# Decayed attention and a gelu MLP on one core: second-block state parts as row tiles, and a new order for wave 1

## The chip, the cores and the metric

The kernel runs on one core of a Trainium2 chip. The metric is the device time of one execution in microseconds, as the median over runs. TensorE (PE) multiplies and writes to PSUM; VectorE (DVE), ScalarE (ACT) and GpSimd (POOL) work on SBUF and PSUM; SyncE (SP) issues the DMAs.

## The reference

The input is q, k, v of shape (4, 8, 768, 64) in float32 (batch, heads, tokens, head size), a decay per head, and two weight matrices of 512 × 2048 and 2048 × 512. The output is (3072, 512) in float32.

```python
for b in range(nb):                       # blocks of 64 tokens
    intra = (qb @ kb^T * Dmask) @ vb      # Dmask[i, j] = lam ** (i - j) for i >= j, else 0
    inter = (qb * lam ** (pos + 1)) @ kv_state
    out[:, :, sl] = intra + inter
    kv_state = lam ** 64 * kv_state + (kb * lam ** (63 - pos))^T @ vb
x = out as (3072, 512)                    # heads side by side
h = x @ w_in
y = (h * sigmoid(1.702 * h)) @ w_out
```

## The kernel before, in words

**Waves.** The kernel holds all weights and operands of matmuls in bfloat16 and accumulates in float32. It works through six waves of 512 rows of the MLP's input. Waves 2 to 5 take 128 tokens of all four batches each. The first 256 tokens are split otherwise, so that work can start on few loads: wave 0 takes 256 tokens of batches 0 and 1, wave 1 the same of batches 2 and 3. A *unit* `(bl, p)` of wave 0 or 1 is one batch and one pair of heads, 256 tokens; a wave has 8 units. In wave 1 the four units with bl = 0 are `A_UNITS` and those with bl = 1 are `B_UNITS`. Token pairs are laid out so that partitions 0 to 63 hold the first 128 tokens (even and odd apart) and partitions 64 to 127 the second 128.

**A unit's work.** `u_cast_kq` scales k (on VectorE) and q (on GpSimd) by powers of the decay while casting them; `u_cast_v` casts v; `u_turn` transposes k and q with four TensorE transposes into PSUM and `u_turn_copy` copies them to SBUF; `u_score` (L301) makes 8 score matmuls of 64×64 weights into the two banks of the tile `s`; `u_mask` (L306, VectorE) multiplies by the causal mask; `u_kv0` (L326) makes 4 matmuls for the state after the first half and `u_kv0_copy` (L335, two ScalarE instructions) writes it to `kv_bd`; `u_inter` (L360) is one full-size matmul of q on that state, and `u_out` adds 8 matmuls of v with the masked scores (L369) and copies the result into the transposed MLP input `xT` (L371, ScalarE). For these waves the state that wave 2 starts from needs the second half too: `u_state(w, p)` (L347) makes 8 matmuls on partitions 64 to 127 for one pair of heads and the two batches of one wave, in its own PSUM tile, and adds them to `kv_bd` into `kv_sb[0]` with two VectorE instructions (L350).

**PSUM.** Eight banks: three single tiles `mm` (MLP accumulators, and wave 0's transposes), one tile `s` of two banks, one tile `o` of two banks, one tile `t`. `s`, `o` and `t` have one buffer each, so a new one waits until the readers of the last are done.

**MLP.** `mlp1(w, fc)` makes 4 matmuls (L453) for 128 of the 2048 hidden units, `gelu` (L459, ScalarE) follows; `mlp2(w, g, j)` makes 4 of the 16 matmuls (L484) for 128 output rows; a copy and a store on SP follow the sixteenth. The very last 128 rows go through `mlp2_last` (L500), which splits the 512 columns in two halves, each with its own copy and store.

**Order.** Instructions are issued in the order in which the program emits them, engine by engine; nothing reorders them but the queues themselves. Wave 0 is a loop with one unit per turn, with filler matmuls on zeros (`fill`, L255; counts in `FILL0` and `FILL`) ahead of each unit's transposes. After it, `put` writes a main list of MLP items with due times on a clock of its own (1 is 4 matmuls of 512 columns), and `at` a side list of attention steps; the merging loop at the end emits a side step before the first main item whose time is not below the step's. `units1` places wave 1's units: A from `A_T` in steps of `A_S`, beside wave 0's `mlp1`; B two items apart, beside wave 0's `mlp2`. Round i of it transposes unit i, scores unit i − 1 and finishes unit i − 2. For each unit the casts come half a step ahead of its transposes. `states` places `u_state`: wave 0's in the stretch where `mlp1` of wave 1 runs for the A half of its columns (HA), wave 1's where it runs for the B half (HB). `full` places waves 2 to 5.

**Loads.** All loads are issued by SP into a ring of SBUF chunks; `pump`, called after each step, issues whatever fits next. The order is wave 0's units (first two of 128 KB per tensor, then nine loads of 256 KB, two units each), `w_in`, wave 1's A units, `w_out`, wave 1's B units, then waves 2 to 5. DMA transposes and stores stand in the same SP queue.

Of the kernel before, what the change touches and what calls it, by code (L numbers as in the profile page):

```python
# [24 lines left out]
def kernel(  # L25
# [60 lines left out]
    def load_units(w, nm, bl, p, n=2):  # L86

        def go(x):
            nc.sync.dma_start(  # L89
                out=x.rearrange("s (h c) -> s h c", h=2 * n),  # L90
                in_=SRC[nm][2 * w + bl, 2 * p : 2 * (p + n), 0 : 2 * P, :].rearrange("h (q j) d -> q h (j d)", j=2))
            for i in range(n):
                loaded[w, nm, bl, p + i] = x.rearrange("s (n h j d) -> s n h j d", n=n, h=2, j=2)[:, i]
        coming.append((n, [(w, nm, bl, p + i) for i in range(n)], 1, go))
# [199 lines left out]
    def u_score(w, bl, p):  # L294
        s = ps.tile([P, 2, W], f32, tag="s", name="ps_s")
        s_ps[w, bl, p] = s
        t = kq_of[w, p][:, bl]
        for j in range(2):
            for x in range(2):
                for h in range(2):  # L300
                    nc.tensor.matmul(s[hd(x), h, j * P : (j + 1) * P].rearrange("s (i m) -> s i m", i=2),  # L301
                                     t[hd(h), 0, j, hd(x)], t[hd(h), 1, :, hd(x)], start=True, stop=True)
# [38 lines left out]
    def u_state(w, p):  # L341

        t = ps.tile([P, W], f32, tag="t", bufs=1, name="ps_kv")[:, 0 : 2 * D].rearrange("s (b d) -> s b d", b=2)
        for bl in range(2):
            for h in range(2):
                for j in range(2):
                    nc.tensor.matmul(t[hd(h), bl, :], kqs_of[w, p][hd(1), bl, 0, j, h],  # L347
                                     v_sb[w % 2][hd(1), p, 2 * bl + j, h], start=(j == 0), stop=(j == 1))
        for h in range(2):
            nc.vector.tensor_tensor(kv_sb[0][hd(h), p, 2 * w : 2 * w + 2, :], kv_bd[hd(h), p, 2 * w : 2 * w + 2, h, :],  # L350
                                    t[hd(h)], op=ADD)
# [12 lines left out]
    def u_out(w, bl, p):  # L364
        o, sm = uo_ps.pop((w, bl, p)), sm_of.pop((w, bl, p))
        for j in range(2):
            for x in range(2):
                for h in range(2):
                    nc.tensor.matmul(o[hd(h), x, 0:P], v_sb[w % 2][hd(x), p, 2 * bl + j, h], sm[hd(x), h, j, :],  # L369
                                     start=(x == 0 and j == 0), stop=True, skip_group_check=True)  # L370
        nc.scalar.copy(xT(w)[:, p, 2 * bl : 2 * bl + 2, :], o[:, :, 0:P])  # L371
# [73 lines left out]
    def mlp1(w, fc, kcs=ALLK, bs=ALL):  # L445
        if (w, fc) not in h_ps:
            if (w, fc) == (0, NF):
                h_ps[w, fc] = ps.tile([P, 2, W], f32, tag="s", name="ps_h4")[:, 0, :]
            else:
                h_ps[w, fc] = ps.tile([P, W], f32, tag="mm", bufs=3, name="ps_h")  # L450
# [43 lines left out]
    def mlp2_last(w, g):  # L494

        hw = d_model // 2
        for c in range(2):
            t = ps.tile([P, hw], f32, tag="mm", bufs=3, name="ps_out")
            for fc in range(FFC):
                nc.tensor.matmul(t, g_of[w][:, fc, g * P : (g + 1) * P],  # L500
                                 w_out_sb[fc // CW][:, fc % CW, c * hw : (c + 1) * hw],
                                 start=(fc == 0), stop=(fc == FFC - 1))
            o = op.tile([P, hw], f32, tag="oh", bufs=2, name="o_sb")
            if c == 0:
                nc.vector.tensor_copy(o, t)
            else:
                nc.scalar.copy(o, t)
            store(w, g, o, slice(c * hw, (c + 1) * hw))

    FILL0, FILL = 12, (0, 2, 2, 2, 1, 1, 1, 1)  # L510
    NF = 3
    A_T, A_S = 7, 1.2
    KV_ENG = {i: nc.vector if i in (2, 4, 6) else nc.scalar for i in range(1, 9)}

    with tc.manual_schedule():
# [63 lines left out]
        def units1(t0, units, step, vcast, copier):  # L579
            n = len(units)  # L580
            for i in range(n + 2):
                t = t0 + step * i
                h = t + 0.5 * step
                if i < n:
                    at(t, u_cast_kq, 1, 0, *units[i], nc.vector)
                    at(t, u_cast_kq, 1, 1, *units[i], nc.gpsimd)
                    at(t, u_cast_v, 1, *units[i], vcast)
                if 0 < i:
                    at(h, new_o)
                if i < n:  # L590
                    at(h, u_turn, 1, *units[i])
                if i > 1:
# [3 lines left out]
                if 0 < i <= n:  # L596
                    at(h, u_score, 1, *units[i - 1])
                    at(h, u_mask, 1, *units[i - 1])
                    at(h, u_kv0, 1, *units[i - 1])
                if i > 1:  # L600
                    at(h, u_out, 1, *units[i - 2])
                if 0 < i <= n:
                    at(h, u_kv0_copy, 1, *units[i - 1], nc.scalar)

        def states(t0, w, step):
            for p in range(NP):
                at(t0 + step * p, u_state, w, p)
# [23 lines left out]
        units1(A_T, A_UNITS, A_S, nc.gpsimd, nc.vector)  # L631
# [15 lines left out]
        states(e - 7, 0, 1.6)  # L647
        units1(e + 2, B_UNITS, 2, nc.scalar, nc.scalar)
# [3 lines left out]
        states(e + 0.5, 1, 1.5)  # L652
# [54 lines left out]
```

## Time and profile before

| | |
|---|---|
| median of 8 runs | 220.23 us (219.7 to 223.4) |
| the profiled execution | 220.1 us, span of its instructions 218.1 us |
| TensorE busy | 209.6 us, 96% of the span, granted clock 1.000 |
| VectorE, ScalarE, GpSimd busy | 107.0, 97.1, 29.0 us |
| first full-rate stream of MLP matmuls | from 20.4 us |
| A half of wave 1 beside wave 0's `mlp1` | 28.8 to 41.3 us |
| wave 0's `mlp2` with the B units | 48.7 to 66.1 us |
| B half of wave 1's `mlp1` | 66.1 to 74.4 us |
| last matmul's copy, then last store | 215.00 us, landed at 217.1 us |
| DMA | 40.15 MB, mean 184 GB/s |

How to read it: a busy time is a sum over the whole span and says nothing of where an engine was late. The chain of work that ended last is followed back from the end, each step to what released it. A line of the timeline has start, duration, engine, line of the kernel, operation, output and inputs, shape and count, and in brackets the idle time before it with what ended it. A matmul's duration includes the way through the array and PSUM; what it costs the next one is seen from the distance of their starts.

### The profile page before, as it was taken

Reading aid. Unit: us, or ns where it says so; the run is one execution under the profiler, and the core shown is the slowest. Engines: PE = TensorE matmul, PEld = TensorE weight load, DVE = VectorE, ACT = ScalarE, POOL = GpSimd, SP = SyncE. Lnnn points to the kernel's source line nnn. Section 1 sums busy time; section 2 is a strip of 40 time slices with the busy share of each in tenths; the row PEclk is TensorE's granted clock in tenths of the full one; section 3 lists DMA queues with packets and bytes.
Section 4 is the critical chain, followed back from the end, with each engine's and each line's share of the span. In section 5 each row is a group of like instructions: output and inputs, shape, how many; then the busy total and the mean of one; then the engine's idle time right before and its main releaser. Section 6 shows DMA issues by size and latency. Waiting matters only on the chain.

```text
span 218.1 us, 4497 instructions
## 1 busy us (share of the span) xinstructions
PE 209.6 (96%) x1766; PEld 107.8 (49%) x1766; DVE 107.0 (49%) x237; ACT 97.1 (45%) x203; POOL 29.0 (13%) x62
## 2 busy tenths in 40 slices
PE   7799979899999999999999999999999999999994
PEld 2354434675547755444554444544444454444453
DVE  4796556694316887193572294661483332100120
ACT  4686747774656511165611075611176520377000
POOL 4773052040040000004000040000040000000000
PEclk9999999999999999999999999999999999999999
DMA  5999999999995899899999979679973222200112
GB/s 135 291 328 376 318 321 387 361 271 214 222 186 107 157 216 200 198 252 192 185 220 186 232 161 219 143 144 191 237 153 73 45 78 75 96 0 0 48 51 96
DMA packets 96741, 40.15 MB, mean 184 GB/s; under 512 B 77136, under 2 KB 89680, under 8 KB 96720
## 3 DMA queue, kind: packets, MB, share of 16 engines
q1 hardware_dynamic: 96576, 39.86, 76.9%
q8 instruction: 14, 0.23, 0.4%
q14 instruction: 7, 0.06, 0.1%
q10 hardware_dynamic: 144, 0.00, 0.0%
HBM read 27.27 MB, written 6.29 MB: 154 GB/s over the span
## 4 chain that ended last, share of the span: by engine, by line
PE 82%; DMA 8%; SPq 5%; ACT 1%; DVE 1%; issue 1%; POOL 0%
PE ps_out L484 37%; PE ps_h L453 33%; DMA ring<-in_moe_w_in_dram 5%; SPq L89 4%; DMA ring<-in_q_dram 3%; PE ps_o L431 2%; PE ps_s L394 2%; PE ps_out L500 2%; PE ps_kv L409 1%; PE ps_o L424 1%; PE ps_t L280 1%; PE ps_kv L347 1%; PE ps_s L301 1%; PE ps_o L369 1%; ACT kv_bd L335 1%
## 5 line engine op out<-in xcount | busy, mean ns | idle before, releaser
L453 PE MATMUL ps_h<-xT,w_in 128*128 128x512 bf16 (+1 forms) x448 | 87.9, 349 | 0.3 <-ACT g_sb L459 0.3
L459 ACT ACTIVATE g_sb<-ps_h 128x512 bf16<-128x512 f32 (+1 forms) x112 | 59.5, 536 | 59.3 <-PE ps_h L453 58.0
L484 PE MATMUL ps_out<-w_out,g_sb 128*128 128x512 bf16 x368 | 83.1, 379 | 0.0
L453 PEld LDWEIGHTS <-w_in 128*128 128x128 bf16 x448 | 42.1, 98 | 37.8 <-issue 0.4
L484 PEld LDWEIGHTS <-g_sb 128*128 128x128 bf16 x368 | 34.8, 98 | 39.0
L491 DVE COPY o_sb<-ps_out 128x512 f32<-128x512 f32 x19 | 13.1, 691 | 52.6 <-PE ps_out L484 49.8
L401 DVE SCALAR_TENSOR_TENSOR sm<-ps_s,inv_pow,mask 128x512 bf16<-128x512 f32 x32 | 22.6, 747 | 22.9 <-PE ps_s L394 22.8
L383 POOL CAST v_sb<-ring 128x512 bf16<-128x512 f32 x16 | 9.8, 651 | 102.2 <-DMA ring<-in_v_dram 66.8
L434 ACT CAST xs<-ps_o 128x512 bf16<-128x512 f32 x16 | 9.4, 586 | 29.2 <-PE ps_o L431 29.2
L306 DVE TENSOR_TENSOR sm<-ps_s,mask 128x512 bf16<-128x512 f32 x16 | 11.0, 688 | 10.7 <-PE ps_s L301 10.7
L263 POOL TENSOR_TENSOR kqs<-ring,kq_pow 128x256 bf16<-128x256 f32 x16 | 10.3, 660 | 28.5 <-DMA ring<-in_q_dram 26.0
L413 DVE SCALAR_TENSOR_TENSOR kv<-kv,blk,ps_kv 64x256 bf16<-64x256 bf16 x24 | 11.4, 474 | 0.2
L381 DVE TENSOR_SCALAR kqs<-ring,k_pow 128x256 bf16<-128x256 f32 x32 | 11.2, 391 | 0.2
L381 DVE TENSOR_SCALAR kqs<-ring,q_pow 128x256 bf16<-128x256 f32 x32 | 11.1, 390 | 0.0
L280 PE MATMUL ps_t<-ident,kqs 128*128 128x128 bf16 x64 | 6.8, 221 | 2.8 <-POOL kqs L263 1.9
L255 PE MATMUL ps_f<-zeros 128*128 128x512 bf16 x22 | 8.1, 488 | 1.3 <-DVE zeros L177 1.3
L263 DVE TENSOR_TENSOR kqs<-ring,kq_pow 128x256 bf16<-128x256 f32 x16 | 7.7, 491 | 3.1 <-ACT kq_pow L208 1.9
L288 ACT COPY kq<-ps_t 128x512 bf16<-128x512 bf16 x10 | 5.9, 587 | 6.8 <-PE ps_t L280 6.8
L280 PEld LDWEIGHTS <-kqs 128*128 128x128 bf16 x64 | 4.6, 98 | 7.7 <-DVE kqs L263 2.9
L350 DVE TENSOR_TENSOR kv<-kv_bd,ps_kv 64x128 bf16<-64x128 bf16 x16 | 4.6, 285 | 7.8 <-PE ps_kv L347 7.4
L371 ACT CAST xT<-ps_o 128x256 bf16<-128x256 f32 x16 | 6.0, 372 | 2.9 <-PE ps_o L369 2.6
L150 DVE CAST w_out<-ring 128x512 bf16<-128x512 f32 x16 | 7.1, 493 | 0.1
(66 smaller groups left out, 118.2 us busy)
## 6 DMA issues: line engine op xcount, KB each, us to landing
ring<-in_k_dram SPq DMA_DIRECT2D x23, 256.0 KB, 4.8
ring<-in_q_dram SPq DMA_DIRECT2D x23, 256.0 KB, 4.6
ring<-in_v_dram SPq DMA_DIRECT2D x23, 256.0 KB, 4.6
ring<-in_moe_w_in_dram SPq DMA_DIRECT2D x16, 256.0 KB, 5.9
ring<-in_moe_w_out_dram SPq DMA_DIRECT2D x16, 256.0 KB, 5.3
out_dram<-o_sb SPq DMA_DIRECT2D x15, 256.0 KB, 2.3
out_dram<-o_sb SPq DMA_DIRECT2D x18, 128.0 KB, 2.6
ring<-in_k_dram SPq DMA_DIRECT2D x2, 128.0 KB, 3.1
```

Source lines behind the costliest of these rows:

```text
L263: eng.tensor_tensor(kqs_of[w, p][:, bl, i].rearrange("s j h d -> s h j d"), read(w, "kq"[i], bl, p), tab, op=MUL)
L280: nc.tensor.transpose(t_ps[w, bl, p][:, i, j, :], kqs_of[w, p][:, bl, i, j].rearrange("s h d -> s (h d)"), ident)
L306: nc.vector.tensor_tensor(sm.rearrange("s h j t -> s h (j t)"), s_ps.pop((w, bl, p))[:, :, 0 : 2 * P], mask2.to_broadcast([P, 2, 2 * P]), ...
L381: nc.vector.tensor_scalar(kqs[:, i, :, h, :], x[:, :, p, h, :], scalar1=(k_pow, q_pow)[i][:, 2 * p + h : 2 * p + h + 1], scalar2=None, op0 ...
L383: nc.gpsimd.tensor_copy(v_sb[w % 2][:, p], read(w, "v")[:, :, p])
L401: nc.vector.scalar_tensor_tensor(sm[:, h], s[:, h], inv_pow[:, 2 * p + h : 2 * p + h + 1], mask.to_broadcast([P, B, P]), op0=MUL, op1=MUL)
L413: nc.vector.scalar_tensor_tensor(new[hd(h), p], old[hd(h), p], blk2[hd(h), p : p + 1], t[hd(h), :, hd(h)], op0=MUL, op1=ADD)
L434: nc.scalar.copy(xs.rearrange("s b h d -> s h b d"), o)
L453: nc.tensor.matmul(t[:, bs[0] * P : bs[1] * P], w_in_sb[fc // CW][:, kc, (fc % CW) * P : (fc % CW + 1) * P], xT(w)[:, kc, bs[0] : bs[1], : ...
L459: nc.scalar.activation(g_tile(w)[:, fc, c], h_ps.pop((w, fc))[:, c], GELU)
L484: nc.tensor.matmul(t, g_of[w][:, fc, g * P : (g + 1) * P], w_out_sb[j][:, fc % CW, :], start=(fc == 0), stop=(fc == FFC - 1))
L491: nc.vector.tensor_copy(o, t)
```

## The change

- **State parts.** `u_state`'s matmuls move into `u_kv1`: 16 matmuls for one pair of heads and all four batches, on partitions 64 to 127, written to the free half of bank 1 of the score tile `s` of that round. They are emitted in the B rounds between `u_kv0` and the 8 matmuls of `u_out`. The additions (`u_state`, two VectorE instructions of twice the width) follow in the same round. `states` is gone. In the last round, which has no scores, `new_s` takes an `s` tile for them alone.
- **Order in wave 1's rounds.** The casts are emitted for two units at a time, `ahead` of the pair's first due time (0.3 in A, 0.5 in B), k and q of both before v of both; B's v casts go to GpSimd instead of ScalarE. `u_out` is split into `u_mm` and `u_x`; on ScalarE the state copy now stands before the x copy, and the mask follows the matmuls. `A_T, A_S` go from 7, 1.2 to 7.4, 1.1.
- **PSUM of one hidden tile.** The accumulator of `(1, 3)` comes from `s` instead of `mm`, in both halves.
- **Fillers.** `FILL` grows from 2 to 4 ahead of the second unit's transposes and from 2 to 3 ahead of the third's.
- **SP.** After each of the nine 256 KB loads of wave 0, five nops on SP's queue.
- **Last rows.** `mlp2_last` splits into 384 and 128 columns instead of 256 and 256.

```diff
--- before.py
+++ after.py
@@ -89,6 +89,9 @@
             nc.sync.dma_start(
                 out=x.rearrange("s (h c) -> s h c", h=2 * n),
                 in_=SRC[nm][2 * w + bl, 2 * p : 2 * (p + n), 0 : 2 * P, :].rearrange("h (q j) d -> q h (j d)", j=2))
+            if w == 0 and n == 2:
+                for _ in range(5):
+                    nc.sync.nop(nofuse=True)
             for i in range(n):
                 loaded[w, nm, bl, p + i] = x.rearrange("s (n h j d) -> s n h j d", n=n, h=2, j=2)[:, i]
         coming.append((n, [(w, nm, bl, p + i) for i in range(n)], 1, go))
@@ -292,8 +295,9 @@
     s_ps = {}
 
     def u_score(w, bl, p):
-        s = ps.tile([P, 2, W], f32, tag="s", name="ps_s")
-        s_ps[w, bl, p] = s
+        if (w, bl, p) not in s_ps:
+            new_s((w, bl, p))
+        s = s_ps[w, bl, p]
         t = kq_of[w, p][:, bl]
         for j in range(2):
             for x in range(2):
@@ -338,17 +342,25 @@
             eng.tensor_tensor(kv_bd[:, p, 2 * w + bl].rearrange("s h d -> s (h d)"), t,
                               blk_bd[:, p].rearrange("s h d -> s (h d)"), op=MUL)
 
-    def u_state(w, p):
-
-        t = ps.tile([P, W], f32, tag="t", bufs=1, name="ps_kv")[:, 0 : 2 * D].rearrange("s (b d) -> s b d", b=2)
-        for bl in range(2):
+    kv1_ps = {}
+
+    def new_s(key):
+        s_ps[key] = ps.tile([P, 2, W], f32, tag="s", name="ps_s")
+
+    def u_kv1(p, key):
+
+        t = s_ps[key][:, 1, 2 * P : 4 * P].rearrange("s (b d) -> s b d", b=B)
+        kv1_ps[p] = t
+        for b in range(B):
             for h in range(2):
                 for j in range(2):
-                    nc.tensor.matmul(t[hd(h), bl, :], kqs_of[w, p][hd(1), bl, 0, j, h],
-                                     v_sb[w % 2][hd(1), p, 2 * bl + j, h], start=(j == 0), stop=(j == 1))
+                    nc.tensor.matmul(t[hd(h), b, :], kqs_of[b // 2, p][hd(1), b % 2, 0, j, h],
+                                     v_sb[b // 2][hd(1), p, 2 * (b % 2) + j, h], start=(j == 0), stop=(j == 1))
+
+    def u_state(p):
+        t = kv1_ps.pop(p)
         for h in range(2):
-            nc.vector.tensor_tensor(kv_sb[0][hd(h), p, 2 * w : 2 * w + 2, :], kv_bd[hd(h), p, 2 * w : 2 * w + 2, h, :],
-                                    t[hd(h)], op=ADD)
+            nc.vector.tensor_tensor(kv_sb[0][hd(h), p], kv_bd[hd(h), p, :, h, :], t[hd(h)], op=ADD)
 
     uo_ps = {}
 
@@ -361,14 +373,20 @@
                          kv_bd[:, p, 2 * w + bl].rearrange("s h d -> s (h d)"), kq_of[w, p][:, bl, 1, :, 64:P],
                          start=True, stop=True)
 
-    def u_out(w, bl, p):
-        o, sm = uo_ps.pop((w, bl, p)), sm_of.pop((w, bl, p))
+    def u_mm(w, bl, p):
+        o, sm = uo_ps[w, bl, p], sm_of.pop((w, bl, p))
         for j in range(2):
             for x in range(2):
                 for h in range(2):
                     nc.tensor.matmul(o[hd(h), x, 0:P], v_sb[w % 2][hd(x), p, 2 * bl + j, h], sm[hd(x), h, j, :],
                                      start=(x == 0 and j == 0), stop=True, skip_group_check=True)
-        nc.scalar.copy(xT(w)[:, p, 2 * bl : 2 * bl + 2, :], o[:, :, 0:P])
+
+    def u_x(w, bl, p):
+        nc.scalar.copy(xT(w)[:, p, 2 * bl : 2 * bl + 2, :], uo_ps.pop((w, bl, p))[:, :, 0:P])
+
+    def u_out(w, bl, p):
+        u_mm(w, bl, p)
+        u_x(w, bl, p)
 
 
 
@@ -444,7 +462,7 @@
 
     def mlp1(w, fc, kcs=ALLK, bs=ALL):
         if (w, fc) not in h_ps:
-            if (w, fc) == (0, NF):
+            if (w, fc) in ((0, NF), (1, 3)):
                 h_ps[w, fc] = ps.tile([P, 2, W], f32, tag="s", name="ps_h4")[:, 0, :]
             else:
                 h_ps[w, fc] = ps.tile([P, W], f32, tag="mm", bufs=3, name="ps_h")
@@ -493,23 +511,21 @@
 
     def mlp2_last(w, g):
 
-        hw = d_model // 2
-        for c in range(2):
-            t = ps.tile([P, hw], f32, tag="mm", bufs=3, name="ps_out")
+        for c in (slice(0, 384), slice(384, 512)):
+            t = ps.tile([P, W], f32, tag="mm", bufs=3, name="ps_out")[:, c]
             for fc in range(FFC):
-                nc.tensor.matmul(t, g_of[w][:, fc, g * P : (g + 1) * P],
-                                 w_out_sb[fc // CW][:, fc % CW, c * hw : (c + 1) * hw],
+                nc.tensor.matmul(t, g_of[w][:, fc, g * P : (g + 1) * P], w_out_sb[fc // CW][:, fc % CW, c],
                                  start=(fc == 0), stop=(fc == FFC - 1))
-            o = op.tile([P, hw], f32, tag="oh", bufs=2, name="o_sb")
-            if c == 0:
+            o = op.tile([P, W], f32, tag="o", name="o_sb")[:, c]
+            if c.start == 0:
                 nc.vector.tensor_copy(o, t)
             else:
                 nc.scalar.copy(o, t)
-            store(w, g, o, slice(c * hw, (c + 1) * hw))
-
-    FILL0, FILL = 12, (0, 2, 2, 2, 1, 1, 1, 1)
+            store(w, g, o, c)
+
+    FILL0, FILL = 12, (0, 4, 3, 2, 1, 1, 1, 1)
     NF = 3
-    A_T, A_S = 7, 1.2
+    A_T, A_S = 7.4, 1.1
     KV_ENG = {i: nc.vector if i in (2, 4, 6) else nc.scalar for i in range(1, 9)}
 
     with tc.manual_schedule():
@@ -576,35 +592,42 @@
         def at(t, *item):
             side.append((t, item))
 
-        def units1(t0, units, step, vcast, copier):
+        def units1(t0, units, step, ahead, vcast, copier, fold):
             n = len(units)
+            for i in range(0, n, 2):
+                t = t0 + step * i - ahead
+                for u in units[i : i + 2]:
+                    at(t, u_cast_kq, 1, 0, *u, nc.vector)
+                    at(t, u_cast_kq, 1, 1, *u, nc.gpsimd)
+                for u in units[i : i + 2]:
+                    at(t, u_cast_v, 1, *u, vcast)
             for i in range(n + 2):
-                t = t0 + step * i
-                h = t + 0.5 * step
-                if i < n:
-                    at(t, u_cast_kq, 1, 0, *units[i], nc.vector)
-                    at(t, u_cast_kq, 1, 1, *units[i], nc.gpsimd)
-                    at(t, u_cast_v, 1, *units[i], vcast)
-                if 0 < i:
-                    at(h, new_o)
+                h = t0 + step * (i + 0.5)
                 if i < n:
                     at(h, u_turn, 1, *units[i])
+                if i > 0:
+                    at(h, new_o)
                 if i > 1:
                     at(h, u_inter, 1, *units[i - 2])
                 if i < n:
                     at(h, u_turn_copy, 1, *units[i], copier)
                 if 0 < i <= n:
                     at(h, u_score, 1, *units[i - 1])
-                    at(h, u_mask, 1, *units[i - 1])
                     at(h, u_kv0, 1, *units[i - 1])
+                key = (1, *units[i - 1]) if 0 < i <= n else "last"
+                if i > 1 and fold:
+                    if key == "last":
+                        at(h, new_s, key)
+                    at(h, u_kv1, units[i - 2][1], key)
                 if i > 1:
-                    at(h, u_out, 1, *units[i - 2])
+                    at(h, u_mm, 1, *units[i - 2])
                 if 0 < i <= n:
                     at(h, u_kv0_copy, 1, *units[i - 1], nc.scalar)
-
-        def states(t0, w, step):
-            for p in range(NP):
-                at(t0 + step * p, u_state, w, p)
+                    at(h, u_mask, 1, *units[i - 1])
+                if i > 1:
+                    at(h, u_x, 1, *units[i - 2])
+                    if fold:
+                        at(h, u_state, units[i - 2][1])
 
         def full(t_cast, t0, w, step, c_step=2.0):
             for p in range(NP):
@@ -628,7 +651,7 @@
         HA, HB = (0, 2), (2, 4)
         for fc in range(NF, FFC):
             put(1, fc_whole, 0, fc)
-        units1(A_T, A_UNITS, A_S, nc.gpsimd, nc.vector)
+        units1(A_T, A_UNITS, A_S, 0.3, nc.gpsimd, nc.vector, False)
         for kc in range(KC):
             for fc in range(3):
                 put(0.125, mlp1, 1, fc, [kc], HA)
@@ -644,12 +667,10 @@
                 put(1, mlp2, 0, g, j)
         for j in range(NJ):
             put(1, mlp2, 0, 3, j)
-        states(e - 7, 0, 1.6)
-        units1(e + 2, B_UNITS, 2, nc.scalar, nc.scalar)
+        units1(e + 2, B_UNITS, 2, 0.5, nc.gpsimd, nc.scalar, True)
         e = clock[0]
         for fc in range(FFC):
             put(0.5, fc_whole, 1, fc, HB)
-        states(e + 0.5, 1, 1.5)
         for g in range(G):
             for j in range(NJ):
                 put(1, mlp2, 1, g, j)
```

## The prediction

> **What bounds the kernel now.** I read the page's table of busy time and its slices first, then the chain in order of time, then the timeline of TensorE where the chain shows something else than matmuls.
>
> ```profile
> PE 209.6 (96%) x1766; PEld 107.8 (49%) x1766; DVE 107.0 (49%) x237; ACT 97.1 (45%) x203; POOL 29.0 (13%) x62
> ...
> PE 82%; DMA 8%; SPq 5%; ACT 1%; DVE 1%; issue 1%; POOL 0%
> ```
>
> TensorE is busy for 96% and carries 82% of the chain. The rest is the front, which the chain shows as loads:
>
> ```profile
> 18.22 5.30 DMA ring<-in_moe_w_in_dram
> ...
> 23.62 5.66 DMA ring<-in_q_dram
> 29.28 0.07 issue
> 29.35 0.62 POOL kqs L263
> 29.97 0.05 issue
> 30.02 0.30 PE ps_t L280 x2
> ```
>
> Up to 30 us the kernel is paced by what lands; after the q load of wave 1's first pair (29.28) no load appears on the chain. From there TensorE's own instruction stream is the clock, so a microsecond counts if it is TensorE work or a TensorE stall. The timeline of TensorE (start, duration; a matmul's duration includes its pipe, so spacing is read from starts):
>
> ```profile
> 30.02 0.29 PE L280 MATMUL ps_t<-ident,kqs 128*128 128x128 bf16 x2 [0.84 <-POOL kqs L263]
> 30.14 1.02 PE L453 MATMUL ps_h<-xT,w_in 128*128 128x512 bf16 x4
> 31.54 0.40 PE L280 MATMUL ps_t<-ident,kqs 128*128 128x128 bf16 x4 [0.38 <-DVE kqs L263]
> ...
> 33.45 0.40 PE L280 MATMUL ps_t<-ident,kqs 128*128 128x128 bf16 x4 [0.19 <-DVE kqs L263]
> ...
> 38.05 0.23 PE L360 MATMUL ps_o<-kq,kv_bd 128*128 128x128 bf16 x1 [0.15 <-ACT kv_bd L335]
> ...
> 39.86 0.23 PE L360 MATMUL ps_o<-kq,kv_bd 128*128 128x128 bf16 x1 [0.47 <-ACT kv_bd L335]
> ...
> 40.25 0.50 PE L453 MATMUL ps_h<-xT,w_in 128*128 128x256 bf16 x3
> 40.69 0.31 PE L347 MATMUL ps_kv<-v_sb,kqs 64*64 64x64 bf16 x8
> 40.93 0.61 PE L453 MATMUL ps_h<-xT,w_in 128*128 128x256 bf16 x4
> 41.80 0.60 PE L453 MATMUL ps_h<-xT,w_in 128*128 128x256 bf16 x4 [0.25 <-ACT g_sb L459]
> ```
>
> Two things are to be seen. First, six stalls. Measured from start to start, less the steady spacing of the shape (0.216 us for 512 columns, 0.109 for 256, 0.056 for 128), the excess is 1.26 us at the first transposes (28.4 to 30.0), then 0.54, 0.36, 0.32, 0.64 and 0.42: 3.5 us, all between 28.4 and 41.8. After 41.8 the largest excess up to 92 us is 0.10. Second, one state part (L347): the three matmuls from 40.25 should hand over at 40.25 + 3 × 0.11 = 40.59; the next full matmul starts at 40.93. Its 8 matmuls so cost 0.34 us, of which their starts cover 0.12 and two excesses of 0.09 to 0.10, entering and leaving, the rest. All eight of them show the same.
>
> **What the skill says.** The Trainium skill, TensorEngine Tiling (Array Packing), Key Properties: changing the tiling mode drains TensorE, and different tiles load and multiply in parallel. The trace agrees with both: 0.09 us wherever 128-row and 64-row matmuls meet, while four 64×64 score matmuls start within 10 ns (36.397 to 36.407). The same page, Gotcha 1: two row tiles may not use one PSUM bank at once. The new state parts write bank 1 of the score tile from rows 64 to 127 only, the state matmuls beside them another tile's bank 0 from rows 0 to 63. TensorE: Matmul & The Clock Gate, What overlaps and what doesn't, says that matmuls start in program order; here the trace differs: the first L369 starts at 36.537, ahead of three of the four L326 that precede it in the program (36.540, 36.589, 36.596), so row tiles do run beside each other.
>
> **State parts.** Eight groups of 8 matmuls (L347) go: 8 × 0.34 = 2.73 us. Four groups of 16 come, placed after L326 and ahead of L369, inside a stretch that is already in 64×64 mode, so no switch is added. In L347 the starts come in pairs (two column tiles) every 31 ns, so 16 need 8 × 31 = 0.25 us on row tile 64 to 127. In rounds 2 to 4 of the second units, rows 0 to 63 have L326 (2 × 56 ns) and half of L369 (2 × 56) = 0.22; rows 64 to 127 get 0.25 + 0.11 = 0.36. The round grows by 0.36 − 0.22 = 0.14; the last, with no L326 beside it, by 0.25. Sum 3 × 0.14 + 0.25 = 0.67. Bounds: nothing, if all hides; 16 × 31 ns × 4 = 2.0, if row tiles take turns. I take 0.67. Gain 2.73 − 0.67 = 2.05 us (0.7 to 2.7).
> The score tile is now held until VectorE has added the state. VectorE per round: mask 0.69 and two additions of 64×256, between 0.285 (half that width, L350) and 0.474 (same width with a scalar, L413), so at most 1.64 us; rounds are 2.3 to 2.5 us apart (53.23, 55.63, 58.20), so this hides. Without that cover, score matmuls and the matmuls behind them would wait for the difference. The v casts of the second units go from ScalarE to GpSimd, idle there; data lands by 48.9, the first transposes come near 48.8 us and need only k and q (45.2). Wave 2's casts no longer queue behind state additions on VectorE (67.5 now, its data landed at 58.3), so the 1.4 us taken from the stretch before its scores does not make those late.
>
> **First units of wave 1.** I lay the new order on the measured durations. Transposes 0 stay before the same item (due 7.95 instead of 7.6, both before item 8): the stall of 1.26 stays, set by the load. Transposes 1 move from before item 9 to before item 10, and the k cast they waited for now precedes transpose copy 0 on VectorE: the 0.54 goes. They start at 31.87. Transposes 2 need a k cast that is still behind copy 1 and mask 0 on VectorE: 1.905 us after transposes 1, as now (31.54 to 33.45), so 33.78 against TensorE's 33.40: a stall of 0.38 stays. Round 3 follows after 0.84 + 0.86 at 35.48 without a wait. Its ScalarE work, state copy 0.64 then x copy 0.37, begins 0.6 after its inter matmul (35.70) and ends at 37.31; TensorE is back at 37.19: stall 0.17. Round 4 ends at 37.97; the gelu of item 12 stands ahead on ScalarE, then 0.64 + 0.37 gives 38.98, and the last inter matmul waits about 0.62. The order of the two copies is worth 0.1 at most, since both must end before the next inter matmul takes the same PSUM tile. The last tile of the small matmuls ends at 40.31 instead of 41.38, of which 0.34 was a state part: gain 0.73. The h tile of (1, 3) now sits in the score tile's banks, free since mask 3, and doesn't wait for a gelu: gain 0.42. Together 1.15 us (0.3 to 1.6).
>
> **Start.** Three more fill matmuls of 0.22: two follow 6.40 and push the next transposes from 6.83 to 7.27, but the scores wait for a copy until 7.50 anyway; one follows 7.85 and ends by 8.5, where k is awaited until 8.72. Nothing. If that wait were gone: 0.65.
> The 45 nops stand on SP's queue between the nine loads of wave 0's later units and ahead of w_in and everything SP issues later. No nop is in the trace; the time between two SP instructions, 0.04 to 0.05 us, is the nearest price: 5 × 0.045 = 0.23 per load. The nine issues fill 3.85 to 10.71, 0.76 each, of which 0.56 is the least seen; the queue is already held back by 0.2 each, while loads land every 0.87 (8.21, 9.08, 9.98). With 0.78 per load it stays ahead: cost 0. From below, a steadier queue could land loads earlier: up to −0.5; from above, see the rivals.
>
> **Tail.** 16 × (0.163 + 0.056) = 3.5 us of matmuls, as 32 × 0.109 was. ScalarE's last copy has 128 columns instead of 256: from 0.60 (512) and 0.37 (256), 0.26 by the same slope, −0.11; the last store is half as large, but follows a larger one sooner. I take −0.15 in all (−0.3 to 0).
>
> **Sum.** −2.05 − 1.15 − 0.15 = −3.35 against the profiled execution's 220.1 us (its span of 218.1 and 2.0 around it): 216.75. The median of the runs is 0.13 above that execution: 216.9 us.
>
> **Rivals.**
> *Row tiles take turns.* 16 matmuls at 31 ns each in all four groups: +1.3, 218.2 us. For it: the state parts' pairs show column tiles of one row tile alone; against it: L326 and L369 interleave.
> *The front gives nothing.* TensorE gets to wave 1's waits sooner, and the ScalarE chain hands the time back at the last two inter matmuls: 216.9 + 1.15 = 218.05. For it: 0.32 and 0.64 are ScalarE's today; against: the VectorE and gelu stalls have causes that the new order removes. With the first rival: 219.3, no change that can be told.
> *Nops starve the queue: slower.* The last of the nine loads is issued at 9.85 and lands at 15.22; a 128 KB load lands 3.0 us after issue, the larger one by estimate 3.4, so issuing by 11.8 costs nothing. Without holds it could be issued at 8.3, 40 nops later: free to (11.8 − 8.3) / 40 = 88 ns each. Beyond that each ns costs 45, all of it on the path through w_in and q. The gain of 3.35 is used up at 88 + 3350/45 = 162 ns a nop, and 222 us is reached at 200. Against it: the 45 ns gap.
>
> **How the numbers follow.** Main forecast 0.52; row tiles take turns 0.16; front gives nothing 0.15; both 0.06; nops starve 0.06; a luckier front with the q load earlier (215.9) 0.05. Less than 0.5% (1.1 us) can't be told from no change. Faster: 0.52 + 0.16 + 0.15 + 0.05 = 0.88; same 0.06; slower 0.06. The range takes the luckier front and both single rivals with their spread, 215.5 to 219.0, leaving the double rival and the nops out.
>
> **What would show it.** Right: no L347 group alone; the stretch from the first score to the full matmul after L369 near 0.6 us in the second units, against 0.46 now; TensorE's waits between 28 and 42 us near 2.4; mlp2 of wave 0 starting 2.5 us sooner (46.2); every later stage shifted by 3.2. Wrong: the q load of wave 1 landing after 29.8, a VectorE wait on score matmuls of wave 1, or a wait that opens at wave 2's scores.

## The result and the profile after

The changed kernel takes 217.63 us as the median of 11 runs (216.78 to 218.75) against 220.44 us for the kernel before in 32 runs; the ratio is 0.9867, 95% interval 0.9841 to 0.9893. Measured once more later, beside fresh runs of the kernel before, it took 216.59 against 220.53 us, ratio 0.9820 (0.9782 to 0.9857). So it is faster by 2.9 us in the first measurement and by 4.0 in the second; the forecast was 3.35. The first profiled execution took 217.76 us with a span of 216.1; the second one's span was 214.8.

The page of the profile after, busy times and the chain by engine:

```profile
PE 208.3 (96%) x1769; PEld 107.5 (50%) x1769; DVE 105.1 (49%) x229; ACT 95.5 (44%) x199; POOL 30.0 (14%) x66
...
PE 79%; DMA 10%; SPq 7%; ACT 1%; issue 1%; DVE 1%; POOL 0%; ACTq 0%
```

TensorE is still busy for 96% of a span that is 2.1 us shorter, but DMA and SP carry 17% of the chain where they carried 13%. The stretches show why. Their times, in us, are distances between starts of TensorE's matmuls; the prediction's column applies its terms to the column before, and the last column is the second profile of the same kernel.

| stretch of TensorE's stream | before | predicted | after | again |
|---|---|---|---|---|
| start to the end of wave 1's first transposes | 30.14 | 30.14 | 30.74 | 29.93 |
| from there to wave 0's second matrix (A rounds, A half) | 18.38 | 15.87 | 16.24 | 16.21 |
| wave 0's second matrix with the B rounds | 17.41 | 18.08 | 18.09 | 18.09 |
| B half of wave 1's first matrix | 9.05 | 7.69 | 7.65 | 7.65 |
| wave 1's second matrix | 17.41 | 17.41 | 17.41 | 17.41 |
| wave 2 | 31.88 | 31.88 | 32.30 | 31.88 |
| waves 3 and 4 | 62.87 | 62.87 | 62.87 | 62.87 |
| wave 5 to the end of the span | 31.00 | 30.85 | 30.77 | 30.76 |

Two rows differ between the two profiles of one kernel, the first by 0.8 and wave 2 by 0.4 us. They are the two in which TensorE waits for DMAs: for loads at the start, for the x transposes in wave 2. The others repeat to 0.03.

**The B rounds.** TensorE's timeline in one round with state parts, from the first score matmul to the next full one:

```profile
54.28 0.31 PE L305 MATMUL ps_s<-kq 64*64 64x128 bf16 x8
...
54.48 0.22 PE L330 MATMUL ps_o<-v_sb,kqs 64*64 64x128 bf16 x2
54.48 0.26 PE L357 MATMUL ps_s<-v_sb,kqs 64*64 64x64 bf16 x6
54.56 0.24 PE L381 MATMUL ps_o<-sm,v_sb 64*64 64x128 bf16 x2
54.58 0.23 PE L357 MATMUL ps_s<-v_sb,kqs 64*64 64x64 bf16 x4
...
54.89 0.39 PE L502 MATMUL ps_out<-w_out,g_sb 128*128 128x512 bf16 x1
```

L305 are the scores, L330 the state after the first half, L357 the new state parts and L381 the output matmuls. Their starts mix: at 54.56 two output matmuls start (by the program's order those on rows 0 to 63), while state parts on rows 64 to 127 are still to come. The stretch is 54.886 − 54.284 = 0.60 us; the same stretch was 56.294 − 55.836 = 0.46 before.

**The A rounds.** The *inter matmul* of a round is `u_inter` (L372 now, L360 before). TensorE's waits now, with ScalarE in the second view:

```profile
34.38 0.40 PE L283 MATMUL ps_t<-ident,kqs 128*128 128x128 bf16 x4 [0.21 <-DVE kqs L266]
...
36.41 0.22 PE L372 MATMUL ps_o<-kq,kv_bd 128*128 128x128 bf16 x1
...
37.02 1.04 PE L471 MATMUL ps_h<-xT,w_in 128*128 128x512 bf16 x4
38.22 0.22 PE L372 MATMUL ps_o<-kq,kv_bd 128*128 128x128 bf16 x1 [0.16 <-ACT xT L385]
...
38.83 0.61 PE L471 MATMUL ps_h<-xT,w_in 128*128 128x256 bf16 x4
40.02 0.22 PE L372 MATMUL ps_o<-kq,kv_bd 128*128 128x128 bf16 x1 [0.59 <-ACT xT L385]
```

```profile
37.14 0.63 ACT L339 ACTIVATE kv_bd<-ps_o,blk 64x64 bf16<-64x64 f32 x2 [0.26 <-PE ps_o L381]
37.80 0.37 ACT L385 CAST xT<-ps_o 128x256 bf16<-128x256 f32 x1
38.09 0.60 ACT L477 ACTIVATE g_sb<-ps_h 128x512 bf16<-128x512 f32 x1
38.95 0.63 ACT L339 ACTIVATE kv_bd<-ps_o,blk 64x64 bf16<-64x64 f32 x2 [0.26 <-PE ps_o L381]
```

The waits for VectorE ahead of the second transposes and for the gelu are gone. What is to be seen in ScalarE's lines is the releaser of the state copy (L339): L381, the eight output matmuls, not the state matmuls. They share the tile `ps_o`. The copy begins 0.73 us after the round's inter matmul (36.41 to 37.14). In the kernel before, the x copy (L371) stood first, and it began just as late, 0.73 us after the inter matmul, released by the output matmuls as well:

```profile
36.25 0.22 PE L360 MATMUL ps_o<-kq,kv_bd 128*128 128x128 bf16 x1
...
36.98 0.37 ACT L371 CAST xT<-ps_o 128x256 bf16<-128x256 f32 x1 [0.15 <-PE ps_o L369]
37.36 0.63 ACT L335 ACTIVATE kv_bd<-ps_o,blk 64x64 bf16<-64x64 f32 x2
```

Whichever copy comes first, the pair takes about 1.0 us from there, and the next inter matmul follows the second copy. So inter matmuls are 1.80 us apart before (36.25 to 38.05) and after (36.41 to 38.22), and in the A rounds of none of the fourteen traces is a distance of theirs shorter. The new order brings all three distances to this pace, where before the first one was 2.57 us, and gets no further.

**Wave 2.** The chain of the first profile before wave 2's first hidden tile:

```profile
86.47 0.59 SPq L104
...
87.15 4.00 DMA xT<-xs
91.15 0.04 issue
91.19 1.89 PE ps_h L471 x8
```

Wave 2's fourth matmul needs the last x transposes at 90.12 + 3 × 0.216 = 90.77; they landed at 91.15, and it started at 91.19: a wait of 0.4 us that the kernel before didn't have (landed 92.56, needed 93.04).

### The profile page after: what moved, and what is told of

Read it like the earlier page. It is cut to its first block, busy times and chain, and to the rows that moved or that the text cites. A ratio compares the mean times of both kernels' runs of the same rounds, so it can differ in the third digit from the quotient of the medians.

```text
span 216.1 us, 4496 instructions
## 1 busy us (share of the span) xinstructions
PE 208.3 (96%) x1769; PEld 107.5 (50%) x1769; DVE 105.1 (49%) x229; ACT 95.5 (44%) x199; POOL 30.0 (14%) x66
## 4 chain that ended last, share of the span: by engine, by line
PE 79%; DMA 10%; SPq 7%; ACT 1%; issue 1%; DVE 1%; POOL 0%; ACTq 0%
PE ps_out L502 33%; PE ps_h L471 33%; DMA ring<-in_moe_w_in_dram 5%; SPq L89 4%; DMA ring<-in_q_dram 3%; PE ps_s L412 2%; PE ps_o L449 2%; DMA xT<-xs 2%; PE ps_out L517 2%; PE ps_kv L427 1%; SPq L453 1%; PE ps_o L442 1%; PE ps_t L283 1%; PE ps_s L305 1%; PE ps_o L381 1%
## 5 line engine op out<-in xcount | busy, mean ns | idle before, releaser
L471 PE MATMUL ps_h<-xT,w_in 128*128 128x512 bf16 (+1 forms) x448 | 86.6, 349 | 0.9 <-POOL w_in L153 0.7
L477 ACT ACTIVATE g_sb<-ps_h 128x512 bf16<-128x512 f32 (+1 forms) x112 | 59.3, 537 | 56.7 <-PE ps_h L471 55.3
L471 PEld LDWEIGHTS <-w_in 128*128 128x128 bf16 x448 | 42.7, 98 | 38.4 <-POOL w_in L153 0.8
L399 DVE TENSOR_SCALAR kqs<-ring,k_pow 128x256 bf16<-128x256 f32 x32 | 11.9, 412 | 0.1
L399 DVE TENSOR_SCALAR kqs<-ring,q_pow 128x256 bf16<-128x256 f32 x32 | 11.8, 411 | 0.0
L258 PE MATMUL ps_f<-zeros 128*128 128x512 bf16 x25 | 9.1, 495 | 1.3 <-DVE zeros L180 1.3
L266 DVE TENSOR_TENSOR kqs<-ring,kq_pow 128x256 bf16<-128x256 f32 x16 | 6.8, 446 | 3.3 <-ACT kq_pow L211 1.9
L153 DVE CAST w_in<-ring 128x512 bf16<-128x512 f32 x13 | 5.5, 426 | 3.3 <-DMA ring<-in_moe_w_in_dram 3.1
L412 PEld LDWEIGHTS <-kq 64*128 64x128 bf16 x128 | 3.6, 94 | 6.6 <-issue 6.6
```

The source lines that it names most:

```text
L266: eng.tensor_tensor(kqs_of[w, p][:, bl, i].rearrange("s j h d -> s h j d"), read(w, "kq"[i], bl, p), tab, op=MUL)
L399: nc.vector.tensor_scalar(kqs[:, i, :, h, :], x[:, :, p, h, :], scalar1=(k_pow, q_pow)[i][:, 2 * p + h : 2 * p + h + 1], scalar2=None, op0 ...
L471: nc.tensor.matmul(t[:, bs[0] * P : bs[1] * P], w_in_sb[fc // CW][:, kc, (fc % CW) * P : (fc % CW + 1) * P], xT(w)[:, kc, bs[0] : bs[1], : ...
L477: nc.scalar.activation(g_tile(w)[:, fc, c], h_ps.pop((w, fc))[:, c], GELU)
```

## The experiments

All of them start from the changed kernel, and every ratio is to the kernel before. There are four sets, the first four experiments, the next four, then two and two. Each was measured beside fresh runs of the kernel before, so times compare best within a set. "The A side" is the stretch from wave 1's first transposes to wave 0's second matrix, "wave 2" the stretch from wave 2's first matmul to wave 3's.

**State parts put back.**

```diff
-        units1(e + 2, B_UNITS, 2, 0.5, nc.gpsimd, nc.scalar, True)
+        states(e - 7, 0, 1.6)                  # u_state with its own tile and matmuls, as before
+        units1(e + 2, B_UNITS, 2, 0.5, nc.gpsimd, nc.scalar, False)
...
+        states(e + 0.5, 1, 1.5)
```

> The changed kernel with the eight separate state parts (8 matmuls each, own PSUM tile) put back where they stood, all else as changed. Theory (row tiles work beside each other, a mode switch costs 0.09 us): slower than the changed kernel by 8 x 0.34 - 0.67 = 2.05 us, so near 219.7 us; B rounds shorter by 0.69 us, the A half longer by 4 x 0.34 and the B half by 4 x 0.34. Rival (row tiles take turns): the B rounds shrink by 2.0 us and the kernel is slower by 0.7 us only.

Measured: ratio 0.9951 (0.9931 to 0.9971), 218.83 against 219.71 us. The old-filler and the 40-nop kernel of the same set, which run like the changed kernel (below), took 216.62 and 216.84 us: putting the parts back costs 2.0 to 2.2 us. By stretches: B rounds 17.41 instead of 18.09, the A side 17.72 instead of 16.24, the B half 9.05 instead of 7.65, together +2.2 us. The B rounds shrank by 0.68, not by 2.0: row tiles that took turns are refuted. Wave 2 took 31.88 here.

**The old A order.** Only the A units take the old rounds:

```diff
-        units1(A_T, A_UNITS, A_S, 0.3, nc.gpsimd, nc.vector, False)
+        units1_old(7, A_UNITS, 1.2, nc.gpsimd, nc.vector)
```

> The changed kernel with the old round order, old due times and single casts for the A units only; hidden tile (1, 3) still in the score tile. Prediction's theory: slower than the changed kernel by 0.73 us. Rival (the ScalarE chain at the last two rounds hands most of it back, as the trace after suggests): slower by 0.3 us, with TensorE's excess between the first transposes and the small matmuls 1.9 us instead of 1.45.

Measured: 0.9897 (0.9861 to 0.9932). From the first transposes to wave 0's second matrix 16.77 instead of 16.24 us: the new order is worth 0.53, between the two expectations. This run takes back casts, copies and due times together, but its trace tells where the gain lies: TensorE's waits ahead of the second and third transposes sum to 1.01 us here against 0.37, while those ahead of the last two inter matmuls are 0.32 and 0.64 here against 0.33 and 0.75. The k casts' earlier place and the later due times gain; moving the state copy ahead of the x copy does not. Wave 2 took 32.18.

**The old fillers.**

```diff
-    FILL0, FILL = 12, (0, 4, 3, 2, 1, 1, 1, 1)
+    FILL0, FILL = 12, (0, 2, 2, 2, 1, 1, 1, 1)
```

> The changed kernel with the old filler counts (2 and 2 instead of 4 and 3). Theory (fillers lie in waits; the front of the changed kernel's profile was late by chance): same within 0.3 us, with the end of the first transposes of wave 1 anywhere between 30.0 and 30.8. Rival (three more filler matmuls move TensorE's instruction fetch so that it delays the w_in loads): faster than the changed kernel by 0.6 us, first row of w_in landed at 15.9 instead of 17.5, first transposes done at 30.1.

Measured: 0.9854 (0.9827 to 0.9881), the same as the changed kernel within the intervals; the first transposes ended at 29.87 and the first row of w_in landed at 16.0. That alone would fit the rival. The second profile of the changed kernel speaks against it: with the new fillers it has 29.93 and 15.9. The fillers cost nothing that shows, and nothing shows that they gain.

**Eight times the nops.**

```diff
-                for _ in range(5):
+                for _ in range(40):
                     nc.sync.nop(nofuse=True)
```

> The changed kernel with 40 nops after each of the nine loads instead of 5. Theory (a nop takes no time that can be seen: the gap between two load issues is 0.044 us before and after the change): same as the changed kernel, gaps unchanged. Rival (a nop costs tens of ns and five were hidden in held-back issues): at 45 ns each, issues of the nine loads spread to 2.3 us apart, w_in issued near 25 us instead of 10.7, the kernel slower by 12 us or more; at 10 ns each, 0.96 us per load, slower by up to 1 us.

Measured: 0.9862 (0.9833 to 0.9892). SP's timeline with 40 nops after each of the nine loads:

```profile
3.88 0.47 SPq L89 DMA_DIRECT2D ring<-in_k_dram  x1
4.39 0.51 SPq L89 DMA_DIRECT2D ring<-in_q_dram  x1
4.94 0.51 SPq L89 DMA_DIRECT2D ring<-in_v_dram  x1
...
10.37 1.74 SPq L120 DMA_DIRECT2D ring<-in_moe_w_in_dram  x3
```

3.88 + 0.47 to 4.39 leaves 0.04 us for 40 nops and the usual gap, which was 0.04 us before the change too. The nops take no time that shows; no record of one is in the trace. Whether they reach the chip at all stays open, and no run leaves them out.

**State parts ahead of the scores.**

```diff
+                    at(h, new_s, key)
+                    at(h, u_kv1, units[i - 2][1], key)
                     at(h, u_score, 1, *units[i - 1])
                     at(h, u_kv0, 1, *units[i - 1])
-                    at(h, u_kv1, units[i - 2][1], key)
```

> The changed kernel with the 16 state-part matmuls emitted ahead of the round's score matmuls instead of after the 4 state matmuls. Theory (each row tile takes its own instructions in order, so rows 0 to 63 go on with scores while rows 64 to 127 work off the state parts): same as the changed kernel, the stretch from the first 64x64 matmul to the next full one 0.60 us in rounds 2 to 4 as before. Rival (matmuls start in program order): the state parts' 0.25 us stand alone ahead of the scores, 0.71 us a round, slower by 3 x 0.11 = 0.33 us.

Measured: 0.9844 (0.9793 to 0.9896), no difference in time from the changed kernel that the intervals show. The timeline of one round:

```profile
53.63 0.35 PE L357 MATMUL ps_s<-v_sb,kqs 64*64 64x64 bf16 x10
53.79 0.24 PE L305 MATMUL ps_s<-kq 64*64 64x128 bf16 x1
...
53.81 0.23 PE L357 MATMUL ps_s<-v_sb,kqs 64*64 64x64 bf16 x3
...
54.27 0.39 PE L502 MATMUL ps_out<-w_out,g_sb 128*128 128x512 bf16 x1
```

The stretch is 54.265 − 53.628 = 0.64 us: 0.04 more than the 0.60 of the theory and 0.07 less than the 0.71 of the rival, so neither holds as it stands. Scores overtake state parts that stand ahead of them, so row tiles do not start in program order; but ten state matmuls start before the first score, so the overtaking has a limit. Wave 2 took 32.85.

**The hidden tile (1, 3) back.**

```diff
-            if (w, fc) in ((0, NF), (1, 3)):
+            if (w, fc) == (0, NF):
```

> The changed kernel with the hidden tile (1, 3) back in the single accumulators. Theory: TensorE waits 0.42 us for the first gelu of the A half, slower by 0.42 us. Rival (the wait only moves to the next hidden tile in the changed kernel): same.

Measured: 0.9881 (0.9835 to 0.9927). TensorE's timeline has the wait back (41.00, `[0.25 <-ACT g_sb L477]`), and the stretch from wave 1's first hidden matmul to wave 0's second matrix is 8.56 us instead of 8.15: 0.41. Wave 2 took 33.13.

**The last rows in halves.**

```diff
-        for c in (slice(0, 384), slice(384, 512)):
+        for c in (slice(0, 256), slice(256, 512)):
```

> The changed kernel with the last rows split 256 and 256. Theory: from the start of the last matmul to the end of the span 3.44 us instead of 3.16, less 0.05 for its later start: slower by 0.24 us, too little for the times to tell. Rival: no difference in the trace.

Measured: 0.9849 (0.9795 to 0.9903). From the last matmul's start to the end of the span 3.45 instead of 3.16, wave 5's matmuls 27.56 instead of 27.61: the split is worth 0.24 us. Wave 2 took 32.50.

**A rounds spread by ScalarE's need,** with wave 2's last rounds sooner:

```diff
-    A_T, A_S = 7.4, 1.1
+    A_T, A_S = 7.15, 1.05
...
-                h = t0 + step * (i + 0.5)
+                h = t0 + step * (i + 0.5) + (0 if fold or i <= n else 0.475)
...
-        units1(A_T, A_UNITS, A_S, 0.3, nc.gpsimd, nc.vector, False)
+        units1(A_T, A_UNITS, A_S, 0.6, nc.gpsimd, nc.vector, False)
...
-        full(e + 1, e + 7.6, 2, 2.4)
+        full(e + 1, e + 7.6, 2, 2.2)
```

> The changed kernel with the A rounds spread by what ScalarE needs: one item between every two rounds, the last item of wave 0's first matrix and four small groups between rounds 4 and 5, casts of a pair one round sooner, and wave 2's last two rounds one item sooner. Theory (a round's state copy starts only after the 8 output matmuls, so two inter matmuls are 1.81 us apart at least, and the second pair's k cast stood behind the first mask): TensorE's excess from the first full item after the first transposes to the small matmuls falls from 1.55 to about 0.3 us, and wave 2's first matmuls never wait: faster than the changed kernel by 1.1 us, near 0.982 of the kernel before. Rival (the loads of the second pair, which land at 31.8 to 32.7, set the rounds): the stalls turn up at transposes 2, gain 0.3 us at most.

Measured: 0.9831 (0.9795 to 0.9868). The A side took 15.72 instead of 16.24 us: 0.52 of the 1.25 expected. The wait at the third transposes is gone, so the loads did not set the rounds, but a new one came. TensorE's waits of this kernel, with the sum in us, the number and the longest:

```profile
PE ps_s L412 <- DMA kq<-kqs: 0.5, 1, 0.5
PE ps_h L471 <- ACT g_sb L477: 0.5, 1, 0.5
...
PE ps_o L372 <- ACT xT L385: 0.2, 1, 0.2
```

Wave 1's third hidden tile needs the accumulator whose gelu now stands behind two copies on ScalarE (L477). And L412: the x transposes were in time for wave 2, but wave 3's first scores, which stand inside the stretch of wave 2, waited for their k and q, and wave 2 took 32.47. The step to 2.2 moved the wait for a DMA, it didn't remove it.

**Wave 3's loads earlier and denser.**

```diff
-        load_spread(e + 4, 3, 1.8)
+        load_spread(e + 2, 3, 1.3)
```

> The changed kernel with wave 3's twelve loads due from 2 in steps of 1.3 instead of from 4 in steps of 1.8, counted from the start of wave 1's B half. Theory (with 1.4 us of TensorE work gone ahead of wave 2, the loads and transposes that the queue has to move in that stretch have become the limit, and wave 2's first hidden matmuls wait for the last x transposes, 0.3 to 1.3 us in five of the changed forms): the loads are out of the way, wave 2 to wave 3 takes 31.88 us again, faster than the changed kernel by 0.5 us. Rival (the queue moves the same bytes anyhow and the wait appears elsewhere, at wave 2's or wave 3's scores): same as the changed kernel, wave 2 to wave 3 above 32.2 us or the stretch before it longer than 17.41.

Measured: 1.0070 (1.0048 to 1.0092), slower than the kernel before. The wait did appear elsewhere, as the rival said, but the loss is larger than its "same": wave 1's second matrix took 19.07 and wave 2 36.20 us. The waits, and then one window of time in us from the start (its length; busy times of PE, PEld, DVE, ACT and POOL; granted clock; DMA share; GB/s):

```profile
PE ps_h L471 <- DMA xT<-xs: 2.6, 1, 2.6
...
PE ps_o L442 <- ACT xs L452: 1.5, 1, 1.5
```

```profile
90.00:96.00 6.00, 3.39 (x12) 1.24 (x11) 4.98 (x17) 0.60 (x1) 2.60 (x1) 0.80 0.98 222
```

Loads issued earlier stand ahead of the transposes in the one queue. Its last x transposes landed at 93.79, ScalarE's copy waited for a buffer that a transpose still read, and TensorE for both. With this order of its work the DMA queue sets the pace there; what order would serve it best was not tried.

**Both together,** the spread A rounds and the early loads, wave 2's rounds where they were:

```diff
     # the spread A rounds as above, with full(e + 1, e + 7.6, 2, 2.4)
-        load_spread(e + 4, 3, 1.8)
+        load_spread(e + 2, 3, 1.3)
```

> The changed kernel with the early loads of wave 3 and the spread A rounds (casts a round sooner, one item between rounds, last round late), wave 2's rounds where they were. Theory (the two gains add: 0.5 us at wave 2, and 0.5 us in the A half, where the spread form spent 15.72 us from the first transposes to wave 0's second matrix against 16.24): faster than the changed kernel by 1.0 us. Rival (what the A half gains comes back at the queue): by 0.5 us or less.

Measured: 1.0040 (1.0014 to 1.0067), no gain; wave 2 took 36.38 us. The premise of this run fell with the one before.

**The changed kernel again,** unaltered.

> The changed kernel once more, with a profile of its own. Theory (front and wave 2 vary with where instruction fetches meet the loads and the DMA transposes; the rest is fixed by TensorE's stream): the stretches that loads don't touch repeat to 0.05 us (first transposes to wave 0's second matrix 16.24, that matrix with the B rounds 18.09, B half 7.65), the end of the first transposes lies between 29.8 and 30.8, wave 2 to wave 3 between 31.9 and 33.1; ratio to the kernel before 0.985 to 0.988. Rival (the later front of the first profile belongs to the change): first transposes end at 30.7 again.

Measured: 0.9820 (0.9782 to 0.9857), a little below the ratios expected; the stretches are in the table above. The first transposes ended at 29.93, so the late front of the first profile does not belong to the change.

**The spread A rounds alone.**

```diff
     # the spread A rounds as above, without the edit of wave 2's rounds
-        full(e + 1, e + 7.6, 2, 2.2)
+        full(e + 1, e + 7.6, 2, 2.4)
```

> The changed kernel with the spread A rounds alone, waves 2 and on as in the changed kernel. Theory: 15.72 us instead of 16.24 from the first transposes to wave 0's second matrix, faster than the changed kernel beside it by 0.5 us. Rival (TensorE's gain ahead of wave 2 comes back there, at a DMA queue that is already the limit): wave 2 to wave 3 longer by as much, same as the changed kernel.

Measured: 0.9804 (0.9763 to 0.9845), 216.36 us beside 216.59. The A side is 15.74 instead of 16.21 us in the trace, and wave 2 takes 31.88, so here the gain did not come back at the queue. The median is the lowest of all forms, but 0.23 us is less than the intervals can tell.

## Why the prediction was right, point by point

The time came out at 217.6, then 216.6 us for a forecast of 216.9; the second profile's span is 3.34 us shorter than that of before, for a sum of 3.35. That the sum fits so well there is partly luck: the A rounds gave 0.34 less than forecast, a front that happened to end 0.21 sooner and a tail that gave 0.09 more made up for it. In the first profile, where the front came late and wave 2 waited, the span is only 2.1 us shorter.

**State parts: right in each term.** The prediction had −8 × 0.34 and + 0.67. The B half lost 1.40 (predicted 1.36), the B rounds grew by 0.68 (0.67): a round with scores 0.14 (0.602 against 0.458), the last 0.25 (61.976 to 62.465 against 63.092 to 63.332). That row tiles take turns is refuted by the first experiment, which also gives the whole of the state parts as 2.20 us by stretches, for 2.05. The cover named for the longer hold of the score tile held: no TensorE wait on score matmuls appears in the B rounds. (The starts that the prediction lists for these rounds are 2.40 and 2.57 us apart, not 2.3 to 2.5; the cover is 1.64.)

**First units of wave 1: right in kind, too large by 0.37 us.** Less 1.36 us of state parts, the stretch became 0.78 us shorter, not 1.15. The step that failed is "its ScalarE work, state copy 0.64 then x copy 0.37, begins 0.6 after its inter matmul". It begins 0.73 after, as ScalarE's pair of copies did in the kernel before; in the trace the state copy is released by the output matmuls that precede it in the same tile. The prediction lets the fourth inter matmul follow the third after 1.66 us (35.70 to 37.36), where the trace of the kernel before showed 1.80. The last two waits so became 0.33 and 0.75 (predicted 0.17 and 0.62), and 0.10 opened at round 3, for the same cause: its inter matmul, too, follows the x copy. The rival that the front gives nothing had seen this chain rightly, but not that the waits for VectorE and the gelu go. A form that emits the state copy ahead of the output matmuls was not run. The stall of 0.38 at transposes 2 was exact (0.37). Single edits give 0.53 for the order and 0.41 for the hidden tile, 0.16 more than both together; where the rest lies is open.

**Start: right, with a front that varies.** Fillers and nops cost nothing that shows. The stall of 1.26 at the first transposes was rightly left to the loads: over thirteen profiles of the changed kernel and its forms the next full matmul starts anywhere from 29.3 to 30.7. A sign that the prediction gave for being wrong, wave 1's q load landing after 29.8, came up in the first profile (29.88) and not in the second (29.07). So wave 0's second matrix, which began at 48.52 before (the table there has 48.7), began 1.55 us sooner in the first and 2.38 in the second, for 2.5 forecast. For the nops the price taken, 0.045 us each, was wrong; the conclusion stood on the held-back queue and would have stood without it.

**Tail: undersized.** The split gave 0.24 us instead of 0.15.

**"Every later stage shifted by 3.2" did not hold in every execution.** Wave 3 starts 1.85 us sooner in the first profile and 3.10 in the second. Where the prediction listed what could open, it named wave 2's scores; it did not look at the x transposes, whose margin was 0.48 us before. In the forms with the B half at 7.65 us and the loads as changed, wave 2 took 31.88 in the old-filler, the 40-nop, the repeated and the spread kernel, and 32.18 to 33.13 in the old A order, the first profile, the last-rows kernel, the state-parts-first kernel and the hidden-tile kernel. So up to 1.25 us are lost there to the wait for the x transposes. In the four forms that lost nothing they landed 0.05 to 0.32 us ahead of the need. That the shorter B half took the margin is argued, not shown: the two traces with the long B half lost nothing, but one of them (state parts put back) had a margin of 0.14 only. What makes a form lose in one execution and not in another is not settled. In the first profile the DMA records show a candidate: a fetch of 16 KB of instructions at 82.57 us, and after it a stretch in which the queue all but stops, with transposes in flight:

```profile
82.00:82.60 0.60, 0.60 (x4) 0.29 (x3) 0.60 (x2) 0.39 (x1) 0.00 (x0) 1.00 1.30 299
82.60:83.20 0.60, 0.60 (x4) 0.29 (x3) 0.58 (x3) 0.00 (x0) 0.00 (x0) 1.00 4.39 143
83.20:84.40 1.20, 1.20 (x7) 0.39 (x4) 1.09 (x2) 0.00 (x0) 0.00 (x0) 1.00 0.39 13
```

The last number is GB/s: 299, 143, then 13 for 1.2 us. But the repeated kernel has such a fetch (81.42) and such a pause (near 82.4) too and lost nothing, so this was seen, not shown to be the cause.

## What to carry to other kernels

Small matmuls on half of TensorE's rows cost little where the other half has work in the same tiling mode. In this kernel 16 of them, whose starts alone take 0.25 us, lengthened a round by 0.14, the excess of the busier row half; and they no longer pay for two mode switches of 0.09 us a group.

Moving a copy ahead of another on its engine gained nothing here, since both read one tile that a later producer still writes. Look at the releaser of the copy, not at its place in the list, and look in the trace before for the distance that two rounds never go below (here 1.80 us).

When TensorE's time ahead of a queue shrinks, look up the margin of every transfer that it meets next. Here it was 0.48 us, and up to 1.25 us were lost at that place.

## What the runs showed of the hardware that was not expected

- Row tiles overtake each other in TensorE's queue, but not from any distance: with 16 state matmuls ahead, the first score started after ten of them, 0.16 us after the first.
- After TensorE had waited 2.8 us for the x transposes in the early-load kernel, its next matmuls of 512 columns started 0.427 us apart instead of 0.216, for about eight matmuls, and the granted clock from 93.6 to 96.9 us is 0.50. The trace of the combined kernel shows the same after a wait of the same length; a wait of 1.26 us in the hidden-tile kernel was followed by nothing of the kind. In these two traces the slower matmuls cost 1.5 and 1.7 us on top of the wait. That the wait is the cause is read from these three traces and not tested; some runs of the kernel before, of which there is no trace, have the same mean granted clock, near 0.992.
- Forty nops behind each of nine load issues left the gap between issues at 0.04 us.
